# One projection product is issued half a step later in an attention and feed-forward kernel

## The chip, the cores and the metric

The kernel runs on one core of one Trainium2 chip. The metric is device time in microseconds (us), the median of several runs. A core has a matrix engine (PE; its weight loads are listed apart as PEld), a vector engine (DVE), an activation engine (ACT), GpSimd (POOL, which here only issues loads) and SyncE (SP, which here issues stores and DMA transposes). Each works through its own list of instructions in order; semaphores tie the lists together.

## The reference

Sliding-window attention with a distance bias, then a gated feed-forward block on the result:

```
scores = q @ k^T / sqrt(64)                      # 8 batches, 8 heads, 576 positions, head size 64
mask   = (0 <= i - j < 128);  bias = -slope[h] * |i - j|
attn   = softmax(where(mask, scores + bias, -1e9))
x      = (attn @ v) as (4608 tokens, 512)
out    = (silu(x @ w_gate) * (x @ w_val)) @ w_out   # w_gate, w_val: 512 x 1536, w_out: 1536 x 512
```

Inputs and output are float32; the kernel multiplies in float16 and adds up in float32.

## The kernel before, in words

Tokens are worked in nine blocks of 512, numbered n = 0 to 8. Attention makes its x ahead of the feed-forward block that needs it: 36 units of 128 queries, two batches (nine units) at a time. The two are woven together in the source by generators. The generator of the feed-forward part yields after every piece of PE work, with a size; the driver adds the sizes up and, at each yield, advances the attention generator until it has reached a target for that sum.

Inside one of the blocks 2 to 5, the loop over m (12 columns of 128 hidden features) has two half steps each: the gate product pg, then the value product pv (both in `wide`, four matmuls of 128 x 512 each, L397). ACT makes tt from pg (L415), DVE makes uu (L416), and DVE multiplies uu by pv into hT (L427). pg and pv share three PSUM banks (tag "gv").

The output projection of block n - 1 is made while block n is worked, by a scheme with seven products instead of eight, in two halves t = 0 and 1 (`strassen`). So a block holds 14 products, each of six matmuls of 128 x 256 (L532), and the set AT names the 14 half steps, of 24, behind which one is issued. The second product of each half writes p2 (p in the profile); the other six go to X and Y, two halves of one bank (po). p2 comes from the pool ps_a, tag "a", which has four banks and is shared with attention. After the second product DVE adds p1s to p2 (L537, into osb), and p2's bank is free.

Attention takes its PSUM from the same four banks. A score group of `scores` (ps, eight matmuls that use 64 rows each, L278) fills all four; ACT reads one bank after the other with an exponential (L284, ex), and DVE multiplies each pair by the mask (L290). `weighted` (av, L345) then takes two banks, one for each half of the heads; DVE reads them (reciprocal L347, multiplication into x, L348). `x_transposed` takes one more (px, L371), which ACT copies (L375).

From step 60 of the driver on, PE's order is that of the source; the orders of DVE and ACT are set by a list scheduler when the kernel is built, and those of POOL by hand. SP issues the transposes of loaded q and k (L239) and the stores (L443). POOL loads v, k and q (L185, L191) and waits where a buffer is still in use: v's buffers are released by the av matmuls.

Of the kernel before, what the change touches and what calls it, by code (L numbers as in the profile page):

```python
# [51 lines left out]
def kernel(  # L52
# [186 lines left out]
        nc.sync.dma_start_transpose(transposed_home(name, rank), t_.rearrange("p h d -> p (h d)"))  # L239

    ex = {}

    def scores(i):

        s, p = units[i]
        def combined(n):
            return scores_128(s, (3, 7, 8)[n], 8, (s, "c", n), msk[n])

        def together(one, two):
            return [one[0] + two[0]] + one[1:] + two[1:]  # L250

        if p == 8:
            first = combined(0) if s == 0 else []
            return first + together(combined(1), combined(2))
        if p == 7 and s == 0:
            return scores_128(s, p, p, (s, p), reg[:, :, 0:P])
        if p == 7:
            return together(scores_128(s, p, p, (s, p), reg[:, :, 0:P]), combined(0))
        if p == 3:
            return scores_128(s, p, p, (s, p), reg[:, :, 0:P], i < FIRST)  # L260
        ks = (9 * s + p) % NK
        banks = []
        early_tile = i < FIRST
        e = epool.tile([P, H, 256], FP16, name="ex", tag="ex", bufs=4)
        ex[(s, p)] = e

        def products():
            for q4 in range(2):
                two = [ps_a.tile([P, 2, 256], FP32, name="ps", tag="a") for _ in range(2)]
                banks.append(two)  # L270
                for par in range(2 if early_tile else 0):
                    o = 4 * q4 + 2 * par
                    nc.tensor.matmul(two[par], idm, bias[:, o:o + 2, :], start=True, stop=False)
                for j in range(2):
                    pair = 2 * q4 + j
                    for par in range(2):
                        rows = slice(64 * par, 64 * par + 64)
                        nc.tensor.matmul(two[par][:, j, :], kT[rows, ks, pair, :],  # L278
                                         qT[rows, p:p + 2, pair, :], start=(j == 0 and not early_tile),
                                         stop=(j == 1))  # L280

        def act(q4, par):
            o = 4 * q4 + 2 * par
            nc.scalar.activation(e[:, o:o + 2, :], banks[q4][par], AF.Exp, scale=scale)  # L284

        def mul(q4):
            if early_tile:
                return
            o = slice(4 * q4, 4 * q4 + 4)
            nc.vector.tensor_mul(e[:, o, :], e[:, o, :], reg[:, o, :])  # L290

        return [[products], [lambda: act(0, 0)], [lambda: act(0, 1), lambda: mul(0)],
                [lambda: act(1, 0)], [lambda: act(1, 1), lambda: mul(1)]]

    def scores_128(s, kt, qt, key, m, early_tile=False):

        ks = (9 * s + kt) % NK
        banks = []
        e = epool.tile([P, H, P], FP16, name="exc", tag="exc", bufs=5)
        ex[key] = e  # L300

        er4 = e.rearrange("k (a par b) q -> k a par b q", a=2, par=2)

        def products():
            banks.extend(ps_a.tile([P, 4, P], FP32, name="psc", tag="a") for _ in range(2))
            for par in range(2 if early_tile else 0):
                nc.tensor.matmul(banks[par].rearrange("k (a b) q -> k a b q", a=2), idm,
                                 bias.rearrange("k (a par b) q -> k a par b q", a=2, par=2)
                                 [:, :, par, :, 0:P], start=True, stop=False)
            for j in range(4):  # L310
                for par in range(2):
                    rows = slice(64 * par, 64 * par + 64)
                    nc.tensor.matmul(banks[par][:, j, :], kT[rows, ks, j, :], qT[rows, qt, j, :],  # L313
                                     start=(j == 0 and not early_tile), stop=(j == 3))

        def act(par):
            nc.scalar.activation(er4[:, :, par], banks[par].rearrange("k (a b) q -> k a b q", a=2),  # L317
                                 AF.Exp, scale=scale)

        return [[products], [lambda: act(0)],  # L320
                [lambda: act(1), lambda: early_tile or nc.vector.tensor_mul(e, e, m)]]
# [107 lines left out]
    def gate_val(n, m):  # L429
        c0 = 384 if (n, m) in acted else 0  # L430
        gate(n, m, wide(n, m, "g"), c0)
        yield
        val(n, m, wide(n, m, "v"), c0)
        yield
# [265 lines left out]
    AT = {1, 3, 4, 6, 7, 9, 11, 13, 14, 15, 17, 18, 20, 22}  # L700

    def ffn():

        for n in range(NBLK):
            if n > 1:
                parts = chain(strassen(n - 1, 0), strassen(n - 1, 1))
            if n == 1:
                for j in range(PRE):
                    for _ in project(0, j, ps_f, "po", 1):
                        yield 1.0  # L710
            if n == SEVEN_FROM:
                break
            for m in range(NMB):
                for half, _ in enumerate(gate_val(n, m)):
                    yield 1.0
                    if n > 1 and 2 * m + half in AT:
                        next(parts)
                        yield 0.75
                    if n > 1:
                        for _ in range(1 + (len(later) > 3)):  # L720
                            if later:
                                later.pop(0)()
                if n == 1:
                    if m in (4, 6, 8, 10):
                        for _ in project(0, m // 2 - 2, ps_f, "po", 1):
                            yield 1.0
                    if m in (4, 6, 8):
                        weight_sums(m // 2 - 2)
                if n > 0 and m >= 9:
                    (at_once if n == 1 and m < 11 else later.extend)(sums(n, m - 9))  # L730
                if n + 1 == SEVEN_FROM:
                    if m == SILU_AT:
                        attention_ends()
                        by_silu.update((n, i) for i in range(m + 1, NMB))
                    if m in (SILU_AT + 1, SILU_AT + 2):
                        later.extend(gate_val_weight_sums(m - SILU_AT - 1))
                    if m == SILU_AT:
                        later.extend(x_sums(n + 1))
            if n > 1:
                assert next(parts, 0) == 0  # L740
        ends = [strassen(NBLK - 1, t) for t in range(2)]
        final = ()
        for n, k, name, which in seven_steps():
            if k == 0 and n > SEVEN_FROM:
                assert next(parts, 0) == 0
                parts = chain(strassen(n - 1, 0), strassen(n - 1, 1))
            if n == SEVEN_FROM and k in (1, 3, 10, 17):
                later.extend(gate_val_weight_sums(2 + (k + 4) // 7))
            yield 0.5
            if k % 3 == 2 and k < 42:  # L750
                next(parts)
                yield 0.75
            if k == 20 and n + 1 < NBLK:
                later.extend(x_sums(n + 1))
            if k == 35:
                later.extend(sums(n, 0))
            if name == "fourth" and which is not None and which[1] > 3:
                if which == (NBLK - 1, 5):
                    at_once(final)
                else:  # L760
                    later.extend(sums(which[0], which[1] - 3))
            if n == NBLK - 1 and k == 40:
                final = sums(n, 2)
                later.append(final.pop(0))
            for _ in range(2 if len(later) > 4 or k >= 39 or k < 7 else 1):
                if later:
                    later.pop(0)()
            if n == NBLK - 1 and k == 41:
                next(ends[0])
                yield 0.75  # L770
        assert next(parts, 0) == 0 and not later

        for t in (1, 0, 1, 0, 0, 0, 1, 0, 0, 1, 1, 1, 1):
            next(ends[t])
            yield 0.75
# [149 lines left out]
    def attention_ends():  # L925
        while att_step():
            pass
        of = supool.tile([P, 1], FP16, name="turn", tag="turn", bufs=1)
        nc.scalar.activation(of, ex[(NSUP - 1, "c", 2)][:, 0, 0:1], AF.Silu)
# [76 lines left out]
```

## Time and profile before

| what | value |
|---|---|
| median of 6 runs | 343.93 us (343.61 to 344.16) |
| the profiled execution's own time | 343.98 us |
| its span, from first to last instruction | 342.2 us |
| granted PE clock | 1.000 |
| DVE, ACT, POOL busy | 277.3, 207.1, 109.6 us |

The span is what the traces show; what lies around it is 343.98 - 342.2 = 1.8 us. A median has to be set against the span with this in between. Busy times of engines overlap, and a busy share is an average over stages: around 120 us all of attention, feed-forward and projection are under way at once, while after 245 us only feed-forward and projection are left. Starts of matmuls in the trace are measured and their ends are modelled, so the time that a group of matmuls takes is best read from the start of the group to the start of the next.

### The profile page before, as it was taken

The numbers are of one execution on the slowest core, as the hardware profiler recorded it, in microseconds if no ns is written. First come the engines' busy times: TensorE is split into PE (matmuls) and PEld (weight loads), VectorE is DVE, ScalarE is ACT, GpSimd is POOL, SyncE is SP. The second block draws the span as 40 slices with busy tenths as digits, with TensorE's granted clock in tenths as the row PEclk, the third lists the DMA queues.
The fourth block names the chain that finished last, engine by engine and source line by source line (L and its number), as shares of the span: only waits on it lengthen the run. The fifth ranks groups of instructions, "written<-read, shape, count | busy, mean of one in ns | idle before, by whom it ended". The sixth has DMA issues, their size and how long they took to land.

```text
span 342.2 us, 7786 instructions
## 1 busy us (share of the span) xinstructions
PE 329.7 (96%) x2983; PEld 218.4 (64%) x2983; DVE 277.3 (81%) x652; ACT 207.1 (61%) x412; POOL 109.6 (32%) x136
## 2 busy tenths in 40 slices
PE   6999989999999999999999999999999999999995
PEld 3484455444456565565665655656788878888884
DVE  6577885999798769998899999999855975775683
ACT  3758676465765666566665647563467666676640
POOL 8968672649675165835008000000000000000000
PEclk9999999999999999999999999999999999999999
DMA  9999999999999999999969912031101101011024
GB/s 154 169 180 175 163 174 146 83 136 164 131 169 155 158 177 156 160 156 148 147 182 101 177 29 84 15 63 47 63 2 61 63 0 64 12 52 63 0 71 116
DMA packets 160038, 37.38 MB, mean 109 GB/s; under 512 B 147329, under 2 KB 155649, under 8 KB 160001
## 3 DMA queue, kind: packets, MB, share of 16 engines
q0 software_dynamic: 118336, 18.62, 84.8%
q1 hardware_dynamic: 40976, 17.64, 28.1%
q10 hardware_dynamic: 688, 0.62, 0.6%
q8 instruction: 23, 0.38, 0.4%
q14 instruction: 15, 0.11, 0.1%
HBM read 37.91 MB, written 9.44 MB: 138 GB/s over the span
## 4 chain that ended last, share of the span: by engine, by line
PE 72%; DVE 15%; ACT 5%; DMA 4%; issue 3%; ACTq 0%; POOL 0%; DVEq 0%
PE po L532 16%; PE pg L397 14%; PE pv L397 13%; PE gX L624 8%; PE gY L624 4%; PE av L345 4%; DMA qn<-in_q_dram 3%; PE ps L278 3%; PE p L532 2%; DVE hT L427 2%; PE gZ L624 2%; ACT ex L284 2%; DVE uu L416 2%; ACT tt L415 2%; DVE ex L290 2%
## 5 line engine op out<-in xcount | busy, mean ns | idle before, releaser
L397 PE MATMUL pv<-xT,wv_sb 128*128 128x512 f16 (+2 forms) x320 | 76.5, 358 | 0.6 <-DVE uu L416 0.3
L397 PE MATMUL pg<-xT,wg_sb 128*128 128x512 f16 (+2 forms) x320 | 75.8, 358 | 0.3 <-DVE xT L373 0.2
L415 ACT ACTIVATE tt<-pg 128x512 f16<-128x512 f32 (+2 forms) x70 | 41.3, 590 | 47.5 <-PE pg L397 46.5
L284 ACT ACTIVATE ex<-ps 128x512 f16<-128x512 f32 x96 | 50.0, 605 | 10.0 <-PE ps L278 10.0
L416 DVE SCALAR_TENSOR_TENSOR uu<-tt,pg 128x512 f16<-128x512 f16 (+2 forms) x69 | 45.8, 664 | 11.3 <-ACT tt L415 11.1
L427 DVE TENSOR_TENSOR hT<-uu,pv 128x512 f16<-128x512 f16 (+2 forms) x70 | 46.5, 664 | 3.0 <-PE pv L397 1.3
L185 POOL DMA_DIRECT2D va<-in_v_dram x40 | 34.4, 870 | 38.1 <-PE av L345 29.0
L397 PEld LDWEIGHTS <-wv_sb 128*128 128x128 f16 x320 | 28.4, 98 | 24.9 <-issue 3.0
L532 PEld LDWEIGHTS <-hT 128*128 128x128 f16 x384 | 37.0, 98 | 11.3 <-issue 1.7
L397 PEld LDWEIGHTS <-wg_sb 128*128 128x128 f16 x320 | 28.2, 98 | 23.2 <-issue 2.1
L191 POOL DMA_DIRECT2D kn<-in_k_dram x39 | 33.3, 858 | 21.3 <-DMA kT<-kn 10.7
L191 POOL DMA_DIRECT2D qn<-in_q_dram x39 | 33.6, 868 | 14.2 <-DMA va<-in_v_dram 7.3
L532 PEld LDWEIGHTS <-S 128*128 128x128 f16 x288 | 27.3, 98 | 8.9 <-issue 1.4
L290 DVE TENSOR_TENSOR ex<-ex,m_reg 128x1024 f16<-128x1024 f16 x42 | 28.7, 685 | 3.0 <-ACT ex L284 3.0
L348 DVE TENSOR_TENSOR x<-av,rec 128x256 f16<-128x256 f32 x72 | 28.7, 419 | 0.4
L532 PE MATMUL po<-T,S 128*128 128x256 f16 x192 | 26.5, 273 | 0.6 <-DVE S L487 0.3
L532 PE MATMUL po<-T,hT 128*128 128x256 f16 x192 | 26.0, 273 | 0.0
L676 DVE TENSOR_TENSOR hT<-s,v 128x512 f16<-128x512 f16 x18 | 7.6, 422 | 18.5 <-ACT s L675 18.5
L317 ACT ACTIVATE exc<-psc 128x512 f16<-128x512 f32 x40 | 21.3, 607 | 1.9 <-PE psc L313 1.9
L345 PEld LDWEIGHTS <-ex 128*128 128x128 f16 x384 | 17.5, 97 | 4.6 <-issue 1.3
L345 PE MATMUL av<-va,ex 128*128 128x65 f16 x384 | 19.3, 193 | 0.7 <-DMA kn<-in_k_dram 0.5
L278 PE MATMUL ps<-qT,kT 64*128 64x256 f16 x192 | 16.7, 272 | 0.4 <-DVE qT L223 0.2
(134 smaller groups left out, 535.5 us busy)
## 6 DMA issues: line engine op xcount, KB each, us to landing
out_dram<-osb SPq DMA_DIRECT2D x32, 256.0 KB, 2.4
va<-in_v_dram POOLq DMA_DIRECT2D x32, 128.0 KB, 8.0
qn<-in_q_dram POOLq DMA_DIRECT2D x31, 128.0 KB, 9.0
kn<-in_k_dram POOLq DMA_DIRECT2D x31, 128.0 KB, 9.2
wg_sb<-in_moe_w_gate_dram POOLq DMA_DIRECT2D x6, 256.0 KB, 7.5
wv_sb<-in_moe_w_val_dram POOLq DMA_DIRECT2D x6, 256.0 KB, 8.1
wo_sb<-in_moe_w_out_dram POOLq DMA_DIRECT2D x2, 768.0 KB, 10.0
kn<-in_k_dram POOLq DMA_DIRECT2D x8, 64.0 KB, 7.0
```

The lines of the kernel that those rows point to most:

```text
L185: nc.gpsimd.dma_start(va[rank][p0:p1, :, 0:D], src)
L191: nc.gpsimd.dma_start(t_[p0:p1], src)
L284: nc.scalar.activation(e[:, o:o + 2, :], banks[q4][par], AF.Exp, scale=scale)
L290: nc.vector.tensor_mul(e[:, o, :], e[:, o, :], reg[:, o, :])
L345: nc.tensor.matmul(av[:, j, :], w, val, start=(n == 0), stop=(n == len(todo) - 1))
L348: nc.vector.tensor_mul(x[:, 4 * half:4 * half + 4, :], av[:, :, 0:D], rec.broadcast_to([P, 4, D]))
L397: nc.tensor.matmul(ps[:, c0:c1], w[:, kb, ms], xT[n][:, kb, c0:c1], start=(kb == 0 and c0 == 0), stop=(kb == NKB - 1 and c1 == 512), skip_ ...
L415: nc.scalar.activation(tt, pg[:, c0:c1], AF.Tanh, scale=0.5)
L416: nc.vector.scalar_tensor_tensor(out=uu, in0=tt, scalar=one if (n, m) == PIN else 1.0, in1=pg[:, c0:c1], op0=ALU.add, op1=ALU.mult)
L427: nc.vector.tensor_mul(hT[n][:, m, c0:c1], acted[(n, m)][1][:, c0:c1], pv[:, c0:c1])
L532: nc.tensor.matmul(dst, a[:, m, cols], b[:, m, :], start=(start and m == 0), stop=(m == HM - 1), skip_group_check=True)
L624: nc.tensor.matmul(dst[:, i, :], w[:, kb, c0 + i * P:c0 + (i + 1) * P], a[:, kb, :], start=(start and i == 0 and kb == 0), stop=(i == 1 an ...
```

## The change

A flag is set whenever a score group is issued, and cleared ahead of each half step. A product that falls due is counted, and issued at once unless it is the second of its half (the number given so far is 1 modulo 7) and a score group has just been issued; then it stays due, and is issued behind the next half step, followed there by any product that has become due too.

```diff
+    scored = [False]
     def products():                     # in scores and in scores_128
+        scored[0] = True
...
+            due, given = 0, 0
             for m in range(NMB):
                 for half, _ in enumerate(gate_val(n, m)):
+                    scored[0] = False
                     yield 1.0
-                    if n > 1 and 2 * m + half in AT:
+                    due += n > 1 and 2 * m + half in AT
+                    while due and not (scored[0] and given % 7 == 1):
                         next(parts)
+                        due, given = due - 1, given + 1
                         yield 0.75
```

In the built instruction streams this touches one of the eight second products of blocks 2 to 5: in block 2, the second product of t = 1. PE's order there was: gate product of m = 7, score group, second product, value product of m = 7, av, third product. It becomes: gate product, score group, value product, second product, av, third product. On DVE the order around it becomes ex (first pair), hT, osb, reciprocal, ex (second pair), x, reciprocal, x, where it was ex (first pair), osb, ex (second pair), hT, reciprocal, reciprocal, x, x. The streams of ACT, POOL and SP are the same, as is the rest of PE and DVE, and no instruction is added or taken away. The first score matmul of the next group is given its waits on other instructions: what stood on the matmul (a DMA) now stands on its weight load, and the matmul names a wait on DVE.

More of the change, by code (lines that the diff above doesn't have):

```diff
@@ L304, in products @@
         def products():
+            scored[0] = True
             banks.extend(ps_a.tile([P, 4, P], FP32, name="psc", tag="a") for _ in range(2))
```

## The prediction

> **What bounds the kernel now.** I read the page first, then PE's waits, then the stretch around the changed place engine by engine, then the chain of waits behind it.
>
> ```profile
> span 342.2 us, 7786 instructions
> PE 329.7 (96%) x2983; PEld 218.4 (64%) x2983; DVE 277.3 (81%) x652; ACT 207.1 (61%) x412; POOL 109.6 (32%) x136
> ...
> PE 72%; DVE 15%; ACT 5%; DMA 4%; issue 3%; ACTq 0%; POOL 0%; DVEq 0%
> ```
>
> PE is busy for 96% of the span and carries 72% of the chain that ended last; DVE is next. Of PE's waits between 56 and 245 us, longest first (us in total, times, longest), these matter:
>
> ```profile
> PE p L532 <- ACT ex L284: 0.7, 1, 0.7
> ...
> PE po L532 <- DVE S L487: 0.3, 1, 0.3
> ```
>
> The longest is a second product (p) that waits for the exponential. There is one such wait, and its place is the changed one. The timeline of PE, then of ACT, DVE and POOL there (start, duration, line, instruction, idle time before it):
>
> ```profile
> 112.53 0.62 PE L313 MATMUL psc<-qT,kT 64*128 64x128 f16 x16
> 113.08 1.04 PE L397 MATMUL pv<-xT,wv_sb 128*128 128x512 f16 x4
> 113.95 0.82 PE L532 MATMUL po<-T,hT 128*128 128x256 f16 x6
> ...
> 118.66 0.61 PE L278 MATMUL ps<-qT,kT 64*128 64x256 f16 x8
> 119.96 0.81 PE L532 MATMUL p<-wo_sb,hT 128*128 128x256 f16 x6 [0.69 <-ACT ex L284]
> 120.61 1.03 PE L397 MATMUL pv<-xT,wv_sb 128*128 128x512 f16 x4
> 121.47 0.89 PE L345 MATMUL av<-va,exc 128*128 128x65 f16 x24
> ...
> 126.42 0.61 PE L278 MATMUL ps<-qT,kT 64*128 64x256 f16 x8
> 126.96 0.83 PE L532 MATMUL po<-T,S 128*128 128x256 f16 x6
> ```
>
> ```profile
> 119.31 2.06 ACT L284 ACTIVATE ex<-ps 128x512 f16<-128x512 f32 x4
> ...
> 120.43 0.69 DVE L290 TENSOR_TENSOR ex<-ex,m_reg 128x1024 f16<-128x1024 f16 x1 [0.29 <-ACT ex L284]
> ...
> 122.83 0.76 DVE L348 TENSOR_TENSOR x<-av,rec 128x256 f16<-128x256 f32 x2
> 124.61 0.69 DVE L416 SCALAR_TENSOR_TENSOR uu<-tt,pg 128x512 f16<-128x512 f16 x1 [1.03 <-ACT tt L415]
> ...
> 122.60 0.88 POOL L185 DMA_DIRECT2D va<-in_v_dram x1 [10.09 <-PE av L345]
> ```
>
> The score group ps has taken all four "a" banks, so p starts only when the first of four exponentials has given one back. PE stands, with pv, av and all the rest queued in order behind it. POOL's next load, after 10 us of waiting, hangs on the av behind that. The chain further on:
>
> ```profile
> 127.49 0.61 ACT ex L284
> ...
> 128.13 0.69 DVE ex L290
> ...
> 142.55 0.39 PE po L532 x2
> ```
>
> From 127.49 to 142.55 the chain leaves PE and runs through DVE; PE waits only 0.31 us at its end. This is where a gain at 120 us could get lost.
>
> **The change, part by part.** *The wait on PE.* Before, ps starts at 118.66 and av at 121.47: 2.81 us. After, the four pv matmuls come first. Their bank was last read by a uu that began at 116.93 and took 0.69, so it is free. A group of eight ps hands over after 0.54 (118.66 + 0.54; the other group: 126.42 to 126.96), pv takes 0.87 to the next start (113.08 to 113.95, also behind a score group), and p takes 0.65 (119.96 to 120.61). So pv starts at 119.20, p at 120.07, av at 120.72. That is 0.54 + 0.87 + 0.65 = 2.06 instead of 2.81, **0.75 us less**. Is p's bank there at 120.07? The first exponential ended at 119.92 and p started 0.04 later, at 119.96: it would now be 0.11 us early. If that margin were missed, the loss is only what it is missed by.
>
> *The av behind it.* It takes the second and third banks. Four exponentials in 2.06 us, one lasting 0.60, stand (2.06 - 0.60) / 3 = 0.49 apart, so they end near 119.91, 120.40, 120.88 and 121.37. av's first half wants its bank at 120.72 (0.32 spare), the second half, twelve matmuls of 0.03 later, at 121.08 (0.20 spare). No new wait. If this cover were gone, the most it could cost is the 0.49 of one more exponential.
>
> *DVE's new order.* The same eight instructions. The pace of each, start to start, is 0.61 for ex, 0.59 for hT, 0.37 for osb. ex starts at 120.43, hT at 121.04 (pv is done at 119.20 + 1.03 = 120.23), osb at 121.63 (p is done at 120.07 + 0.82 = 120.89), the first reciprocal at 122.00 (av's first half is done near 121.3). All inputs are there ahead of DVE, so the eight end where they ended, at 122.83 + 0.76 = 123.59. The next uu is at 124.61 after 1.03 idle, because its pg came late; with PE 0.75 earlier it is due at 123.86, which leaves 0.27 us. This idle time is the cover that makes the reordering cost nothing; a DVE delay up to 0.27 is free, and beyond it counts in full. What is late next: osb, which frees p's bank, ends 0.6 later than before, but that bank is first wanted by the next ps at 126.42 - 0.75 = 125.67. The second ex moves from 121.41 to 122.10; its av is at 128.49.
>
> *Moved past on the queues.* The product issues no DMA; its store follows much later. SP's and POOL's streams are unchanged. POOL's va at 122.60 is released by av, so this batch of loads starts 0.75 earlier too. Transposes of k and q take about 8 us to land, and the newest q that the group at 126.42 reads was issued before 111, so nothing that PE needs is fixed in time by DMA.
>
> *Is the gain kept to the end?* pg, px, ps from 122.85 to 126.42 follow PE without waits, so ps moves to 125.67, the exponential at 127.49 moves with it, and the DVE run that it starts (128.13) as well; its instructions are the same, so the 0.31 wait at 142.55 stays 0.31. From there to 245 us PE shows no wait, and the ones after that are on DVE, which PE itself feeds. So I carry 0.75 whole.
>
> A weight load is a small uncertainty: the trace shows one of p's, 0.10 us, made at 119.19 during the wait. The Trainium skill ("TensorE: Matmul & The Clock Gate", "Step-by-step: what each phase is for") says that a weight load is pulled ahead of running matmuls only where the row groups do not conflict or the background buffer is used. Score matmuls on both row halves might conflict, and the gain would then be 0.65. I set the row above it: pv behind psc started after 0.55 and took 0.87, with its weight loads paid.
>
> **Sum.** 342.20 - 0.75 = 341.45 of span, 1.78 around it, 343.23 against this execution's 343.98. The median shown is 0.05 lower, 343.93, which gives 343.18. The bounds: nothing gained if DVE holds it all (343.93); at most 0.76, from 119.20 to 119.96, as a wait can't give back more than itself (343.17). Nearly all of the evidence stands at the full end, as the chain is fed by PE at every hand-over.
>
> **Rivals.** *The gain is swallowed by DVE.* For it: in the 16.1 us from 126.42 to 142.55 DVE is busy 15.1, and the chain runs on it. If its run starts at its old time, the wait at 142.55 grows from 0.31 to 1.06 and all is given back: 343.93; half of it gives 343.55. Against it: the run begins with an exponential of a ps that PE issues, and DVE is idle by 1.03, 1.07 and 0.29 us just before it.
>
> *DVE gets stuck behind the reciprocal: slower.* In the new order the reciprocal of av's first half stands ahead of the second ex, x and the next uu. It waits for PE, where formerly ex stood there and waited for ACT alone. If av were held (by the third or fourth exponential, or a bank that DVE itself has yet to free), DVE would stand. It costs nothing until the reciprocal's input comes later than 122.00 + 0.27 = 122.27; to be slower than before it must come over 1.02 later than 122.00, and 0.2% slower from 123.71 on. With av held until px's old time of 124.58 the time would be 343.18 + (124.58 - 122.27) = 345.5. Against it: av's banks are free at 120.40 and 120.88.
>
> *It does not do what it says.* The text speaks of blocks 2 to 5, but one of eight products moves; the seven others have no wait to lose. If p still waited at 120.07 for its bank, for instance for the second exponential, it would start at 120.44 and the gain would be 0.38: 343.55. I count this with the swallowed gain.
>
> **How the numbers follow.** Carried whole: 0.74 (own range 342.95 to 343.45, the scatter of the runs shown). Swallowed in part or whole: 0.13. Stuck behind the reciprocal: 0.13. The mark for faster by 0.2%, about what a measurement of this kernel can tell from no change, is 343.93 - 0.69 = 343.24, only 0.06 above the forecast. Of the 0.74, I put 0.55 below the mark, since every price read from rows lies above 0.69, and 0.19 above it by scatter. With 0.13 for the swallowed gain this makes 0.32 for the same; 0.13 for slower. The range 342.9 to 343.95 takes in the first two cases and leaves out the third.
>
> **What would show it.** In the profile after: p without a wait on ex; pv about 0.54 behind ps and av about 2.06 behind ps; POOL's va near 121.85; uu near 123.86 with some 0.3 idle before it; the next ps near 125.67; the wait before po on S L487 still near 0.3; span near 341.45. I am wrong if that last wait has grown, if DVE stands before a reciprocal for more than 0.3, or if PE shows a new wait behind 143 us.

## The result, and the profile after

The median is 343.03 us (342.58 to 343.59, 18 runs) against 343.81 for the kernel before (38 runs). The ratio is 0.9976, with a 95% interval of 0.9970 to 0.9983: 0.8 us, or 0.24%, less. The forecast was 343.18, a ratio of 0.9978.

The first lines of the page of the kernel after, with the chain by engine:

```profile
span 341.1 us, 7787 instructions
PE 329.8 (97%) x2983; PEld 218.5 (64%) x2983; DVE 277.3 (81%) x652; ACT 207.1 (61%) x412; POOL 109.6 (32%) x136
...
PE 76%; DVE 13%; ACT 6%; issue 2%; DMA 1%; ACTq 0%; DVEq 0%
```

PE's busy time is what it was, the span is 1.1 us shorter. Not all of that is the change: the score group in front of it begins at 118.34 us instead of 118.66, so 0.32 us had come in before it. All of it is there in the score group near 99 us already (98.89 instead of 99.21). Over the profiles of this study whose order ahead of that group is the same, it begins between 118.31 and 119.10: scatter of the first 100 us. So traces are compared from that group on.

PE's timeline there in the kernel after (start, duration, line, instruction); the lines have moved by 2 or 3 in the source:

```profile
118.34 0.61 PE L280 MATMUL ps<-qT,kT 64*128 64x256 f16 x8
118.88 1.04 PE L400 MATMUL pv<-xT,wv_sb 128*128 128x512 f16 x4
119.75 0.82 PE L535 MATMUL p<-wo_sb,hT 128*128 128x256 f16 x6
120.41 0.89 PE L348 MATMUL av<-va,exc 128*128 128x65 f16 x24
...
125.35 0.61 PE L280 MATMUL ps<-qT,kT 64*128 64x256 f16 x8
...
140.57 0.60 PE L535 MATMUL po<-T,S 128*128 128x256 f16 x4
141.48 0.39 PE L535 MATMUL po<-T,S 128*128 128x256 f16 x2 [0.31 <-DVE S L490]
```

p has no wait any more. From the group to av it takes 0.54 + 0.87 + 0.66 = 2.07 us, where it took 2.81, and the next group comes 7.01 behind the first instead of 7.76 (126.42 - 118.66). The wait for S at the end of DVE's stretch is 0.31, as before. DVE and POOL in the same place:

```profile
121.31 0.42 DVE L540 SCALAR_TENSOR_TENSOR osb<-p,p1s 128x256 f32<-128x256 f32 x1
121.65 0.17 DVE L350 RECIPROCAL rec<-av 128x4 f32<-128x4 f32 x1
121.74 0.66 DVE L292 TENSOR_TENSOR ex<-ex,m_reg 128x1024 f16<-128x1024 f16 x1
...
123.54 0.69 DVE L419 SCALAR_TENSOR_TENSOR uu<-tt,pg 128x512 f16<-128x512 f16 x1 [0.27 <-ACT tt L418]
...
127.06 0.69 DVE L292 TENSOR_TENSOR ex<-ex,m_reg 128x1024 f16<-128x1024 f16 x1 [0.29 <-ACT ex L286]
...
121.53 0.88 POOL L185 DMA_DIRECT2D va<-in_v_dram  x1 [9.45 <-PE av L348]
```

The first reciprocal follows osb with no idle time, so DVE was not held by av. Ahead of uu DVE stands idle for 0.27 us where it was 1.03. The mask multiplication that starts DVE's long run begins at 127.06, which is 8.72 behind the score group, where it was 128.13 - 118.66 = 9.47: the run starts 0.75 earlier. Seen from the score group, POOL's load comes 121.53 - 118.34 = 3.19 behind, where it was 3.94: the batch of loads moved with PE, by 0.75.

### The profile page after: what moved, and what is told of

It reads as the page before. It is cut to its first block, busy times and chain, and to the rows that moved or that the text cites. A ratio compares the mean times of both kernels' runs of the same rounds, so it can differ in the third digit from the quotient of the medians.

```text
span 341.1 us, 7787 instructions
## 1 busy us (share of the span) xinstructions
PE 329.8 (97%) x2983; PEld 218.5 (64%) x2983; DVE 277.3 (81%) x652; ACT 207.1 (61%) x412; POOL 109.6 (32%) x136
## 4 chain that ended last, share of the span: by engine, by line
PE 76%; DVE 13%; ACT 6%; issue 2%; DMA 1%; ACTq 0%; DVEq 0%
PE po L535 16%; PE pg L400 15%; PE pv L400 14%; PE gX L627 8%; PE av L348 4%; PE gY L627 4%; PE ps L280 3%; PE po L454 2%; PE p L535 2%; DVE hT L430 2%; PE gZ L627 2%; ACT tt L418 2%; ACT ex L286 2%; DVE uu L419 2%; PE px L374 1%
```

## The experiments

All times from traces are taken from the start of the score group at the changed place ("place"): to the next score group, to the fifth one behind it (at 150.08 in the trace of before; the group of 138.43 with eight matmuls is not counted), and to the end of the span. Each ratio is to the kernel before as it was run beside that kernel; its medians there were 343.90 us for e1 to e4, 343.86 for e5 to e7 (one chip) and 344.06 for e8 to e10 (another). A ratio need not equal the quotient of the two medians; in e3 and e8 they differ by 0.0007. So the ratios can be compared down the table, and the medians only within one of these groups.

| kernel | to next | to the one near 150 | to the end | median, us | ratio to before, 95% interval |
|---|---|---|---|---|---|
| before | 7.76 | 31.42 | 223.5 | 343.81 | |
| after | 7.01 | 30.67 | 222.8 | 343.03 | 0.9976 (0.9970 to 0.9983) |
| e1: p in another bank | 7.02 | 30.68 | 222.8 | 343.30 | 0.9980 (0.9971 to 0.9988) |
| e2: after, DVE nearly in its old order | 7.02 | 30.68 | 223.0 | 343.10 | 0.9977 (0.9968 to 0.9986) |
| e3: before, two more on DVE | 7.77 | 31.43 | 223.5 | 343.64 | 0.9999 (0.9990 to 1.0007) |
| e4: after, two more on DVE | 7.02 | 30.68 | 222.9 | 343.07 | 0.9978 (0.9969 to 0.9987) |
| e5: two more waits | 7.76 | 31.42 | 224.0 | 344.37 | 1.0012 (1.0003 to 1.0020) |
| e6: two more in DVE's run | 7.02 | 31.34 | 223.5 | 343.83 | 1.0001 (0.9990 to 1.0011) |
| e7: third product later | 7.01 | 30.53 | 222.7 | 342.86 | 0.9967 (0.9955 to 0.9979) |
| e8: exponential before tt | 7.54 | 31.21 | 223.5 | 343.82 | 1.0000 (0.9989 to 1.0010) |
| e9: three delays | 7.01 | 30.54 | 222.7 | 342.66 | 0.9964 (0.9950 to 0.9977) |
| e10: after, once more | 7.01 | 30.68 | 222.8 | 343.28 | 0.9980 (0.9971 to 0.9989) |

Behind the group near 150 the traces of before and after are alike: 342.2 - 150.08 and 341.1 - 149.01 are both 192.1.

**e1: the wait taken away without moving anything.** The kernel before, with p in a gv bank in that one half:

```diff
-            p2 = (ps_f.tile([P, HC], FP32, name="p2", tag="gv") if seeded
+            p2 = (ps_f.tile([P, HC], FP32, name="p2", tag="gv") if seeded or (n, t) == (1, 1)
```

> The orders of all engines are those of the kernel before; only the PSUM bank of the one second product is taken from the feed-forward banks (gv) instead of the attention banks (a). Bank theory: p no longer waits for the exponential, starts 0.54 us behind the score group and av 2.06 behind it (before: 2.81); 0.75 us less than before, 343.81 - 0.75 = 343.06. Rival, that the new order of PE or DVE brings the gain: the order is the old one, so no gain, 343.8. A value between would mean that the gv banks make a new wait of their own.

PE's timeline:

```profile
118.83 0.61 PE L278 MATMUL ps<-qT,kT 64*128 64x256 f16 x8
119.37 0.83 PE L532 MATMUL p<-wo_sb,hT 128*128 128x256 f16 x6
120.04 1.03 PE L397 MATMUL pv<-xT,wv_sb 128*128 128x512 f16 x4
120.90 0.89 PE L345 MATMUL av<-va,exc 128*128 128x65 f16 x24
```

p stands directly behind the group and does not wait; av comes 2.07 behind. The stretch is that of the kernel after, and so is the ratio within its interval, with the old order on every engine. What cost the time was the bank, not the order.

**e2: the new order on PE, nearly the old one on DVE.** An order edge puts hT behind the second ex. DVE's order is then ex, ex, osb, hT, reciprocal, reciprocal, x, x; in the kernel before osb stood between the two ex:

```diff
             def mul(q4):
...
+            if (s, p) == (2, 0) and q4:
+                behind(mark["hT"], ins)      # mark["hT"]: hT of block 2, m = 7
```

> PE's order is that of the kernel after; DVE's order at the place is put back to ex, ex, osb, hT, reciprocal, reciprocal, x, x. Bank theory: the DVE order is worth nothing, 343.03 as after, 7.01 us from the score group to the next one (before 7.76). Rival, that DVE's order brings the gain or a part: some or all of 0.75 comes back, up to 343.8 and 7.76.

7.02 and 0.9977: with hT and the reciprocals back where they were, the gain is the same, and e1 has it with the old order to the letter. DVE's order is worth nothing that shows.

**e3 and e4: DVE's idle time used up.** In both, the second x multiplication of unit 17 is made three times instead of once, which gives the same values:

```diff
-            nc.vector.tensor_mul(x[:, 4 * half:4 * half + 4, :], av[:, :, 0:D],
-                                 rec.broadcast_to([P, 4, D]))
+            for _ in range(3 if i == 17 and half else 1):
+                nc.vector.tensor_mul(x[:, 4 * half:4 * half + 4, :], av[:, :, 0:D],
+                                     rec.broadcast_to([P, 4, D]))
```

> The kernel before with two more DVE instructions behind the second x of the place (the same x multiplication again, 0.37 us from start to start), in its 1.03 us of idle time. They need 0.74: free, 343.8, and 7.76 us from score group to score group. If DVE were the limit there already, 344.5.

> The kernel after with the same two DVE instructions at the same place, where 0.27 us of idle time is left. By the prediction, what goes beyond 0.27 counts in full: 0.74 - 0.27 = 0.47 more, 343.5, and 7.01 + 0.47 = 7.48 us from score group to score group. Rival: the late uu has slack of its own, since DVE stands idle for 1.06 us again two instructions later and no PE work waits for that uu: free, 343.03 and 7.01.

Free in both. DVE in e4:

```profile
122.94 1.34 DVE L352 TENSOR_TENSOR x<-av,rec 128x256 f16<-128x256 f32 x3
124.20 0.68 DVE L420 SCALAR_TENSOR_TENSOR uu<-tt,pg 128x512 f16<-128x512 f16 x1
124.98 0.69 DVE L431 TENSOR_TENSOR hT<-uu,pv 128x512 f16<-128x512 f16 x1
126.17 0.69 DVE L420 SCALAR_TENSOR_TENSOR uu<-tt,pg 128x512 f16<-128x512 f16 x1 [0.51 <-ACT tt L419]
```

The first uu is late, by 124.20 - 118.42 = 5.78 behind the place instead of 123.54 - 118.34 = 5.20, but the idle time in front of the next uu takes that up (0.51 left of 1.06 in the kernel after), and that uu starts 7.75 behind the place in both. The delay that was free was not 0.27 us but at least 0.27 + 0.58 = 0.85, and PE waited for none of it.

**e5: the wait made twice more.** The kernel before, with the second products of t = 1 in blocks 3 and 4 moved ahead of the gate product that stood between them and a score group:

```diff
-                    if n > 1 and 2 * m + half in AT:
+                    at = 2 * m + half
+                    if n > 1 and at in AT and not (n in (3, 4) and at == 14):
+                        next(parts)
+                        yield 0.75
+                    if n in (3, 4) and at == 13:
                         next(parts)
                         yield 0.75
```

> The kernel before, with two more second products (blocks 3 and 4, t = 1) put directly behind the score group that stood one gate product ahead of them. Bank theory: each waits about 0.7 us for the first exponential and nothing later gives it back, so 2 x 0.75 = 1.5 more than before, 345.3. Rival, that later slack swallows such waits: 343.8.

A miss: 0.5 us more in the trace, a ratio of 1.0012, not 1.5 us. PE at the two places:

```profile
156.72 0.61 PE L278 MATMUL ps<-qT,kT 64*128 64x256 f16 x8
157.80 0.81 PE L532 MATMUL p<-wo_sb,hT 128*128 128x256 f16 x6 [0.46 <-ACT ex L284]
...
194.92 0.40 PE L313 MATMUL psc<-qT,kT 64*128 64x128 f16 x8
195.25 0.83 PE L532 MATMUL p<-wo_sb,hT 128*128 128x256 f16 x6
```

At 194.92 the group has only eight of the small matmuls and takes two banks, not four: p finds a bank and there is no wait. I had not read the group's form. At 156.72 the group is a full one, but p waits 0.46 and not 0.69. The next group follows after 6.64 instead of 6.12 (162.75 - 156.63 before): 0.52 us lost, and the end is later by that. So nothing behind swallowed this wait, but its size differs from place to place. There the first exponential began 0.43 us behind the start of the group (157.15 - 156.72), at the changed place 0.65 (119.31 - 118.66). e8 asks why.

**e6: is DVE's run at its limit?** The kernel after, with the edit of e3 for unit 19 instead of 17.

> The kernel after with two more DVE instructions (0.37 us each from start to start, the second x of the unit two further on, again) inside the run from 126.4 to 141.5 us in which the chain goes through DVE. If that run is at its limit, as the chain says: 0.74 more, 343.77, and the wait of po for S grows from 0.31 to 1.05. If it has room: 343.03 and a wait of 0.31.

PE's wait in e6:

```profile
142.91 0.39 PE L536 MATMUL po<-T,S 128*128 128x256 f16 x2 [0.97 <-DVE S L491]
```

0.97 instead of 0.31, and the stretch to the group near 150 is 31.34 - 30.67 = 0.67 us longer. The pace of the two added instructions in this full queue is 0.34 each (137.10 to 137.44), so they count in full. From 137 us on, where they stand, the run is shown to be at its limit; ahead of that the DVE list of the kernel after shows no idle time from 127.06 on. The gain came through because the start of the run moved.

**e7: the next wait.** The kernel after, with one more exception in the condition:

```diff
-                    while due and not (scored[0] and given % 7 == 1):
+                    while due and not (scored[0] and given % 7 == 1) and (n, 2 * m + half) != (3, 4):
```

> The kernel after with, in addition, the third product of block 3, t = 0 (the po that waits 0.31 us for S) issued half a step later, behind the next value product. If PE's waits there are worth what they show: 0.31 less than after, 342.7, and no wait of po for S. If the DVE run ahead of it sets the pace whatever PE does: a new wait of about 0.3 close behind, 343.03.

Between the two. The wait for S is gone, but the score group behind it is stretched; before, it took 0.61:

```profile
141.75 0.82 PE L535 MATMUL po<-T,S 128*128 128x256 f16 x6
142.50 0.95 PE L280 MATMUL ps<-qT,kT 64*128 64x256 f16 x8
143.39 1.04 PE L400 MATMUL pg<-xT,wg_sb 128*128 128x512 f16 x4
```

Four "a" banks are wanted there, two of them still held by av until DVE's two x (142.25 to 143.01 in this trace) at the end of the run. Inside the group the second matmul starts at 142.73, 0.06 behind the end of the first x (142.25 + 0.42), and the fifth at 143.06, 0.05 behind the end of the second. That these are the banks waited for is read from the times, not tried by itself. The list of waits does not show it, since it lies inside a group of one form.

The account from start to start: from the group of eight small matmuls (137.46 here, 137.37 in the kernel after) to this score group it takes 5.04 us instead of 5.52, which is 0.48 less, and from there to the group near 150 it takes 6.46 instead of 6.12, which is 0.34 more. So 0.14 us is left of 0.48, the same as 30.67 - 30.53. The intervals of e7 and the kernel after overlap (0.9955 to 0.9979 and 0.9970 to 0.9983), so the 0.14 stands on the traces alone.

**e8: what the wait is made of.** The kernel before, with one order edge on ACT:

```diff
             ins = nc.scalar.activation(e[:, o:o + 2, :], banks[q4][par], AF.Exp, scale=scale)
+            if (s, p, o) == (2, 0, 0):
+                behind(mark["tt"], ins)      # mark["tt"]: tt of block 2, m = 7
```

> The kernel before with one order edge on ACT: the first exponential of the group goes ahead of the activation tt of the gate product in front of it. If the 0.69 us wait of p is made of that activation (which holds ACT from 118.82 on, so that the first exponential starts only at 119.31) and the exponential itself, the exponential can start when its bank is full, near 119.1, p waits 0.46 as in block 3 of the two-more-waits kernel, and the time is 0.24 less than before: 343.6, with 7.53 us from score group to score group. If the exponential alone makes the wait: 0.69 and 343.85. If the late tt delays PE through uu: 343.85 or more.

ACT and PE:

```profile
118.78 0.60 ACT L289 ACTIVATE ex<-ps 128x512 f16<-128x512 f32 x1 [0.55 <-PE ps L283]
119.27 0.59 ACT L422 ACTIVATE tt<-pg 128x512 f16<-128x512 f32 x1
...
119.42 0.81 PE L541 MATMUL p<-wo_sb,hT 128*128 128x256 f16 x6 [0.46 <-ACT ex L289]
```

The exponential starts 0.43 behind the start of the group instead of 0.65, p waits 0.46, and the next group comes after 7.54 instead of 7.76: 0.22 less. So of the 0.69 us, 0.23 was the tt of the gate product in front, and 0.46 is left with the exponential first, which cannot begin before PE has filled its bank. The trace keeps the gain up to the group near 150 (31.21 instead of 31.42), and on this chip the median is 343.82 against 344.06; but the ratio to before (1.0000, 0.9989 to 1.0010) leaves a gain of 0.22 open.

**e9 and e10: three delays.** The condition of e7 with `(n, 2 * m + half) not in ((2, 7), (3, 4))`, so that the fifth product of block 2, t = 0, is delayed too; and the kernel after beside it.

> The kernel after with two more products half a step later: the third of block 3, t = 0 (as in the third-product kernel) and the fifth of block 2, t = 0, whose po waits 0.25 us for ACT's p5s. If each wait of PE that ACT makes is worth what it shows and the one in the DVE run about half: 0.25 + 0.15 = 0.4 less than after, 342.63. If the av that moves ahead of the fifth product waits in its place: 342.88.

> The kernel after as it is, as the reference on the same chip for the three-delays kernel: 343.03 beside 343.8 for before.

342.66 against 343.28 on the same chip: all five runs of e9 (342.61 to 342.80) lie below all eleven of e10 (342.99 to 343.47). The added delay shows in the stretch from the score group at 105.22 to the one at 112.02: 6.80 us, where the kernel after takes 112.20 - 105.01 = 7.19. That is 0.39 less for a wait listed as 0.25; with the 0.14 of e7 (30.67 - 30.54 = 0.13 here) the stretches give 0.5 in all. The intervals of the two ratios to before still touch (0.9950 to 0.9977 and 0.9971 to 0.9989), so that e9 is faster than after rests on the stretches and on the runs of this chip.

## Why the prediction was right, point by point

**The wait on PE** was priced at 0.75: measured 0.75 in the stretch (7.76 to 7.01). The three hand-overs came as priced, 0.54, 0.87 and 0.66, for 0.54, 0.87 and 0.65. e1 shows that the bank is the cause.

**The bank at p's new start** was put 0.11 us ahead. p did not wait, nor did av.

**The weight load.** By the rule of the Trainium skill ("TensorE: Matmul & The Clock Gate", "Step-by-step: what each phase is for") I had allowed a gain of only 0.65, should the load not be pulled ahead of score matmuls. 118.34 to 118.88 is the same 0.54 that the other groups take, so nothing came on top of the price. A step of that size is inside it: the four pairs of score matmuls start at 118.34, 118.45, 118.56 and 118.67, so 0.11 apart, and pv starts 0.21 behind the last pair, with its first weight load at 118.87. That the extra 0.10 is this load is likely, but no run tried it. The price was read from hand-overs that had it in, so taking 0.10 off once more would have counted it twice.

**DVE's order** was costed at nothing; e2 shows that. The step "a DVE delay up to 0.27 is free, and beyond it counts in full" was wrong: e4 put in 0.85, 0.58 more than that, and lost nothing. I had named one idle gap as the whole cover. What counts here is whether anyone waits for the late instruction, and the gap of 1.06 behind it still stood in front of the run. The threshold of the rival "stuck behind the reciprocal" hung on that 0.27 and so was too sharp; the reciprocal did not wait, and a held av was not tried.

**The gain carried to the end.** The run on DVE is at its limit (e6), but it begins behind PE, so it moved whole (by 0.75, at 127.06), and the wait behind it stayed 0.31. No new wait of PE is listed behind it. The rival "swallowed" falls for this change: 0.75 at the place, 0.75 near 150, 0.7 at the end. It is not empty, though: in e7, where the order changed at the end of the same run, 0.34 of 0.48 came back as a new wait. The step "from there to 245 us PE shows no wait" holds only for the list of waits: a score group behind it is held up from within, in the kernel before as in the kernel after (the last section has it). The gain passed that group whole, too.

**The sum.** 0.75 was forecast and 0.8 measured, with an interval of 0.6 to 1.0. The profiled executions differ by 343.98 - 342.93 = 1.05, of which 0.32 lies ahead of the place. That the result fell below the mark of 0.2% owes something to scatter: the same kernel once more (e10) has a ratio of 0.9980, which is the mark itself.

## What to carry to other kernels

On an engine that works its list in order, a product whose result bank has just been handed to another group stands until that bank is released. Here this cost 0.75 us: about 0.22 for the activation in front of the exponential (e8), the rest for the exponential. One other product of 0.87 us put in between, or another bank (e1), took all of it away. Before counting on such a wait, or on removing one, read how many banks the group in front takes and what the releasing engine is doing when it comes. Where another engine has no idle time for a stretch, ask which end of the stretch the gain moves: here one that moved its start was kept whole (0.75 of 0.75), and one that only removed a wait at its end was kept in part (0.14 of 0.48, in the one case tried).

## What the runs showed that I had not expected

The idle time that the trace gives in front of a matmul is less than the wait costs, because it is counted from the modelled end of the matmuls ahead, which lies behind the point where the next would have started. A score group is listed with 0.61 us and hands over after 0.54, which is 0.07 less; a value product is listed with 1.03 and hands over after 0.87, which is 0.16 less. The waits differ by as much: the one listed as 0.69 was worth 0.75, and the one listed as 0.46 cost 0.52 (e5), both behind a score group. The one listed as 0.25 stands behind a value product, in the kernel after:

```profile
106.22 1.03 PE L400 MATMUL pv<-xT,wv_sb 128*128 128x512 f16 x4
107.50 0.82 PE L535 MATMUL po<-T,S 128*128 128x256 f16 x6 [0.25 <-ACT p5s L564]
```

It takes 1.28 us from start to start instead of 0.87, so 0.41, and e9 got 0.39 back (with the order changed too). In the same way the wait for S, listed as 0.31, is worth 0.47: four of the six matmuls of 0.11 each start at 140.57, so the fifth was due at 141.01 and came at 141.48. Start to start is the measure.

A wait can hide inside a group of equal matmuls: the score group in e7 took 0.95 us instead of 0.61, and no list of waits names it. The kernel before has such a group without any change:

```profile
181.72 0.91 PE L278 MATMUL ps<-qT,kT 64*128 64x256 f16 x8
```

An x of DVE runs beside it (181.77 to 182.18), as in e7, and it takes 0.91 in the kernel after as well (at 180.65). What it waits for was not tried.
